# A planned instruction order searched again with other prices, and half of a permuting copy's writes in memory order

## The chip, the cores and the metric

The kernel runs on one core of a Trainium2 chip. The metric is device time in microseconds (us) of one execution. A core has five instruction queues that concern us: PE (TensorE, matmuls), DVE (VectorE), ACT (ScalarE), POOL (GpSimd) and SP (SyncE, which here issues DMAs). Each queue runs in order: an instruction whose inputs are late holds up all that stand behind it on the same engine. Queues wait for one another through semaphores.

## The reference

Attention with random features (Performer), then a Fourier mix and an MLP with a residual. All data is 32-bit float; batch 8, 8 heads, 576 rows, head size 64, 128 features, model width 512, MLP width 2048.

```python
def phi(x):                       # for q and k, scaled by D**-0.25
    h = x @ omega.T - sum(x * x) / 2
    return exp(h - max(h)) / sqrt(m)
kv = phi(k).T @ v                 # per head, over the 576 rows
num, den = phi(q) @ kv, phi(q) @ sum(phi(k))
x = num / (den + 1e-6)            # heads side by side: (8, 576, 512)

u = x + real(fft2(x))             # over rows and columns
un = (u - mean(u)) / sqrt(var(u) + 1e-6)
out = u + relu(un @ w_ch1) @ w_ch2
```

The weights come as 64-bit floats and are narrowed on the chip.

## The kernel before

The program has two parts, and each engine runs all of its first part before its second.

The first part interleaves several streams. Three of them are attention: the 32 pairs of heads are dealt to them in turn (`attn`). One pair takes these steps, and they return in the views below by their lines:

- SP loads K, Q (L375, L378) and V (L383). PE transposes the 9 column blocks of 128 (L511); ACT evicts them from PSUM to SBUF as `kqT`, 512 or 128 columns at a time (L521).
- PE multiplies by the features in quarter tiles (L593). DVE takes the negated maximum of each row (L537), and ACT the exponential with it as a bias, 18 instructions of 128x128 for a pair (L554).
- PE forms `kv` (L627), which DVE or ACT evicts (L641, L643).
- PE transposes the query's features (L511 again) in three groups: one column block, four, and four. ACT evicts each group as `qeT` with a permutation of columns, in two instructions (L528): two of 128x64 and four of 128x256 for a pair.
- PE forms numerator and denominator (L674, L682). DVE takes the reciprocals (L691, L692) and then either DVE multiplies in one instruction (L703) or ACT does it in ten small ones (L699).

Beside attention run: the Fourier mix of a batch as soon as its four pairs are done (folds on DVE and POOL at L730 to L766, PE at L786, L796, L836, L847, ACT at L809 and L880, sums at L897 and L898), the narrowing of 32 weight pieces (L436 or L438, then L441 to L454), the MLP on the first four blocks of 128 rows as filler for PE (L1032, L1055), sums of weight parts (L1125, L1183), and the norms of row blocks (`norm_of`, L962 to L976).

The second part does the rest of the MLP with a product scheme that needs fewer multiplications (PE at L1239 and L1419, sums on DVE, POOL and ACT).

What sets the order is neither the order of the source nor a scheduler's priorities. Every stream is a generator that yields `Step` objects before it records instructions. A `Step` names its engine (or two from which one is chosen) and a planned length in us, the events it needs, and the buffers and PSUM banks it takes and gives back. `Listing.run` keeps a planned clock of each engine and picks, again and again, which stream takes its next step; the instructions are then recorded in that order, and each engine's queue has them so. In the first part the picks are not made greedily: they are written out in the string `PICKS`, one character a step. Its value is split by `divmod(…, 36)`: the remainder is the number of the waiting stream that goes next, and the quotient says whether the step takes the engine that the plan thinks is later, where there are two. The planned lengths still decide which of two engines counts as the earlier and which PSUM bank is free first. In the second part there are no picks, and the step that could begin first by the plan, plus its bias, goes next.

The planned lengths are constants in the source. For the eviction of `qeT` and `kqT` by ACT, for example (`order` is given for `qeT` alone):

```python
cost = 0.05 + 0.107 * (j1 - j0) + (0.06 if order else 0.0)
```

The permuted eviction (`evicted`, L515 to L528) walks the group of four column blocks (`j0` of 1 or 5; h, s, t = 4, 2, 16) with one instruction for each value of s. Its loops are column block, h, t, from the outside to the inside. In SBUF a column block is one float apart, t four floats and h 128; in PSUM t is two floats apart, h 32 and a column block 128.

Of the kernel before, what the change touches and what calls it, by code (L numbers as in the profile page):

```python
# [14 lines left out]
AF = mybir.ActivationFunctionType  # L15
# [20 lines left out]
PE, ACT, DVE, POOL, SP, NONE = "pe", "act", "dve", "pool", "sp", "none"  # L36
# [3 lines left out]
class Clock(NamedTuple):  # L40
# [20 lines left out]


PICKS = (
    "ff40d10e3cdaeebfcdfc3ffcedce8dceajii0ii8b8989i9i827fjejPdgfjhjeejhgidgjiih7cTIhdhOhbfgcbbgggbcggggdh"
    "ciecdhjccikdghddceh9k88lk7hb9aOa8khHM97egcagaba77eiieefileeg8Teffddihhddghhi9cdhicgggccicglgdfcchecf"
    "gcb8ji7hih8hebai89ffgj1GeGf66ggbbegdfefaegffOefcH776dahi6jjjTgfjjKe7jfjj6d6gk6ddkgjmddgiiiijdfbgfhhd"
    "jefjifkkbaOlcjmbkk9hkdj89eofppmhlelmpKLbqdppKn7nlllhfgbgkfijidlkgd9fefijb8dR69j7i7jb8kimkjjnajlhhnjh"
    "cjnjhlkihljgighhU9hhSlmijhjfjmfgaa8obo8nm08kk64ba7nMka8i89k7aegghf6bicheghhfd5gccfhbegh5aibhk3ghfb96"
    "4g79lkfcag7hj87iicmblkfadlgkkdjkgjjjkic7ehi8Jj5cllkfcgmiklihji6hlWbmDVf9cbjjmlfod9eejnjkjmndonimbjnF"
    "q587nSieikih7mfcjhcleekgfTgkPKIddehdcklb4cclajOjajiibab56fc998dffec7e6i8fbidbcagg77fbag7hh54Q78ghffd"  # L70
    "jfghegfk5dlccmSmffdieleieddlNegRejjjghfchJkfhjjebjdbfijjSeeedf6cij5h7bidgcicbdih9fejchefh9bjkeJcccee"
    "di55jiji5kh7jMl86aahhkUhj8bg665ehkkiimnieoQijQhihflgl6j5he6jejj9jcbhjmmVLN89i9k96kkfUagiiibbgieiQhg7"
    "9gfhf6d64bigebahabgd5hPcfdgffddi6cgkfdmfnbm8fgjbdddlflehcgo9elnhk9K4n5ol5oRmm4faoadmU985iimiaLlhGifl"
    "8flimlmkmfjjjplrijjknklkmmhmkilkkk8aagaekljq7!pdiRmimjkihpiqnZnc3jhg6jkefpglhgomdfdondommopk99ihip9p"
    "h4g5kplebombnjbjlbnomkpkgmk6a65jVP4im8ig7lemd87lk7ll5lajkfd3j6llb6ai5mbLONgYoll85fghifmblk6lefk5bklk"
    "g7ekGJhiggmkmnhPhebfnlnflki5bmehjiihdekk900iieedigibcfgca486ed28edaffaee6aeP69g66ffcehOdagabh62b8ah9"
    "a88eOdfadIb9dcbd8affaa63cdNd8dd2d6d7dcafehdaab6aeadd946dee276e8bdcb7d7FF7c9b8MKfgab4f8da766hb9ddMfea"
    "fdb7b8gbadd8acbdd76ed5caac78cd6a5O9ac5f9bGdccggaih8cdeeae4g6g76aaeG7efdfed46277e5abd4a71735P98f5gN6h"
    "E2K9d2biiikahb9jfflac94lll92772343h44hh5JPg8g3ce44ec4dKN558835186M97a9ab48aaba8abc2d837a87J2996b664a"
    "d7bde4EaOgfffg5gHgbQfI98cefggeff7abbK3dea4dbbebac4d42fPb82ee9c7645ad8daaef8f9Nd47hhcbhbh12EHh4Q11ddN"  # L80
    "PfPff0g28G428d34239a99c99ca9099J998aaa5156K98879658bcd9c8Ib85678J7808968006aD50482DIH47753289G86ab6b"
    "49874baa3b33366598063886J69F322022246666664D412332010"
)


# [195 lines left out]
def kernel(  # L281
# [10 lines left out]
    nc = tc.nc  # L292
# [183 lines left out]
    uh = [dram.tile([32, 8, DM], F32, name=f"uh{b}") for b in range(B)]  # L476

    def warm():
        yield Step(PE, 2.5, take=("bank",))
        b, ps = got()  # L480
        for _ in range(6):
            nc.tensor.matmul(ps[:, 0:128], lhsT=ur1[:, 0:128], rhs=ur1[:, 0:128])
        yield Step(NONE, give=(b,))

    def first():

        yield Step(NONE, 3.8)
        yield Step(PE, 0.3, take=("bank",))
        b, omps = got()
        nc.tensor.transpose(omps[:, 0:128], om2d, ident[:])  # L490
        yield Step(DVE, 0.2, makes="om2", give=(b,))
        nc.vector.tensor_scalar(om2[:], omps[:, 0:128], SCALE, None, op0=ALU.mult)
# [20 lines left out]
        return dst  # L513

    def evicted(dst, b, j0, j1, makes, order):  # L515
        cost = 0.05 + 0.107 * (j1 - j0) + (0.06 if order else 0.0)
        yield Step(ACT, cost, 0.02, makes=makes + (j0,), give=(b,), bias=0.08)
        ps = psum_of(b)[:, 0 : 128 * (j1 - j0)].rearrange("q (c p) -> q c p", p=128)
        dst = dst[:, j0:j1, :]
        if order is None:  # L520
            nc.scalar.activation(out=dst, in_=ps, func=AF.Copy)  # L521
            return
        h, s, t = order[j0]
        dst = dst.rearrange("q c p -> q (c p)").rearrange("q (h s t c) -> q s c h t", h=h, s=s, t=t)
        ps = ps.rearrange("q c (h t s) -> q s c h t", h=h, s=s)
        for i in range(s):
            of = ps[:, i, ::-1, :, ::-1] if i and j0 else ps[:, i]
            nc.scalar.activation(out=dst[:, i], in_=of, func=AF.Copy)  # L528

    def softmax(n, ts, num, b, es):  # L530

# [183 lines left out]
    def mix(b):  # L715
# [7 lines left out]
        def folds(n):  # L723
# [11 lines left out]
            for dst, src in ((h[:, 0:NL], h[:, 0:NL]), (h[:, NL : NL + 1], x[:, 4:5])):  # L735
                nc.vector.tensor_tensor(
                    out=dst[:, :, 1 : 2 * QD],
# [7 lines left out]
            for dst, o in ((NC3, ALU.add), (1, ALU.subtract)):  # L745
# [4 lines left out]
                    op=o,  # L750
                )
            step = Step(
                {DVE: 1.02, POOL: 2.5},
                makes=("fold", b, n), give=("half",), port=True, bias=-1.41,
            )
            yield step
# [196 lines left out]
    def norm_of(j, t, i, pool, dst):  # L953
# [4 lines left out]
        st = small.tile([P, 6], F32, name="st", tag="st")  # L958
        mv = small.tile([P, 2], F32, name="mv", tag="mv")
        rstd = small.tile([P, 1], F32, name="rstd", tag="rstd")  # L960
        yield Step(DVE, 1.01, bias=-0.23)
        nc.vector.bn_stats(out=st[:], in_=u[:])  # L962
        nc.vector.bn_aggr(out=mv[:], in_=st[:])
        nc.vector.tensor_scalar(rstd[:], mv[:, 1:2], 1e-6, None, op0=ALU.add)  # L964
        yield Step(POOL, 0.85, port=True, bias=-0.18)
        nc.gpsimd.tensor_tensor(rstd[:], rstd[:], mhalf[:], op=ALU.pow)  # L966
        yield Step(DVE, 0.455, port=True)
        nc.vector.tensor_scalar(u[:], u[:], mv[:, 0:1], rstd[:], op0=ALU.subtract, op1=ALU.mult)
# [588 lines left out]
```

## Time and profile before

The program ran in 1197.02 us, the median of three runs (1194.09 to 1198.68). The profiled execution took 1197.83 us.

| | |
|---|---|
| profiled execution | 1197.83 us |
| its span, first to last instruction of the profile | 1196.0 us |
| PE's first matmul of the second part (L1239) | 438.84 us after the start of the span |
| ACT, permuted copies of 128x256 (L528), x128 | 70.4 us busy, mean 732 ns |
| ACT, permuted copies of 128x64 (L528), x64 | 12.8 us busy, mean 294 ns |
| ACT, exponentials (L554), x576 | 163.9 us busy, mean 449 ns; waited 24.8 us for DVE's maximum (L537) |
| granted TensorE clock | 1.00 throughout |

How to read it. PE's busy time counts modelled ends of pipelined matmuls, so that a busy PE is not yet one at its peak; the weight loads (PEld) beside it show more. Busy time of a group is the union of its instructions, and instructions of one engine overlap at their ends: the mean duration of the 128 long copies times 128 is more than their busy time. What an instruction costs its engine is better read as the time from its start to the next one's start. In timelines a row is a run of equal instructions: start, length of the run, engine, line, operation, tiles, count, and in brackets the idle time before it. "Issue" in the chain of waits is time in which the engine waited for nothing that the profile shows.

### The profile page before, as it was taken

How to read it: one execution, taken by the hardware profiler on the slowest of the kernel's cores; microseconds unless marked ns; L12 is line 12 of the kernel's file. 1: busy time of each engine (PE TensorE's matmuls, PEld its weight loads, DVE VectorE, ACT ScalarE, POOL GpSimd, SP SyncE). 2: the span in 40 equal slices, each digit the busy share in tenths (PEclk: the TensorE clock that was granted, in tenths of full speed). 3: DMA queues.
4: the chain of work that ended last, by engine and by line, in shares of the span. 5: the costliest groups of instructions: out<-in, count | busy, mean ns of one | idle time of the engine just before them, and what ended most of it. 6: DMA issues, size and time to landing. Idle time of an engine off the chain costs nothing.

```text
span 1196.0 us, 31842 instructions
## 1 busy us (share of the span) xinstructions
PE 1169.7 (98%) x12765; PEld 1044.3 (87%) x12765; DVE 710.7 (59%) x1508; ACT 486.0 (41%) x1562; POOL 418.3 (35%) x484
## 2 busy tenths in 40 slices
PE   8989999999999999999999999999999999999998
PEld 6778788778868768998998998999899899899898
DVE  5889899796557562672572473374275176267245
ACT  7989899877755112222222222222222222222211
POOL 2444554363453205304314323322421431430421
PEclk9999999999999999999999999999999999999999
DMA  8745856467564342682483384295096086177255
GB/s 257 211 140 179 243 165 187 127 195 223 143 208 147 107 131 93 199 261 79 154 288 97 109 295 135 63 299 177 13 305 198 32 268 200 63 228 248 62 158 196
DMA packets 144708, 205.71 MB, mean 172 GB/s; under 512 B 49072, under 2 KB 58544, under 8 KB 144560
## 3 DMA queue, kind: packets, MB, share of 16 engines
q1 hardware_dynamic: 144064, 203.41, 53.9%
q8 instruction: 101, 1.65, 0.6%
q14 instruction: 47, 0.39, 0.1%
q10 hardware_dynamic: 496, 0.26, 0.1%
HBM read 171.90 MB, written 35.91 MB: 174 GB/s over the span
## 4 chain that ended last, share of the span: by engine, by line
PE 85%; ACT 9%; DVE 3%; issue 1%; DMA 1%; SPq 1%; POOL 0%; DVEq 0%; ACTq 0%; POOLq 0%
PE banks L1239 32%; PE banks L1419 29%; ACT e L554 5%; PE banks L1032 4%; PE banks L1055 4%; PE banks L511 3%; PE banks L593 3%; ACT qeT L528 2%; PE banks L674 2%; PE banks L627 1%; PE banks L972 1%; PE banks L786 1%; PE banks L836 1%; ACT kqT L521 1%; PE banks L796 1%
## 5 line engine op out<-in xcount | busy, mean ns | idle before, releaser
L1225 DVE CUSTOM_DVE_ANT_0 hid<-banks,s 128x256 f32<-128x256 f32 x192 | 79.7, 423 | 255.3 <-PE banks L1239 250.5
L1419 PE MATMUL banks<-wl,sums 128*128 128x128 f32 x1792 | 217.3, 275 | 0.0
L1419 PEld LDWEIGHTS banks<-wl,sums 128*128 128x128 f32 x1792 | 208.8, 192 | 0.4
L1253 ACT ACTIVATE s<-banks 128x256 f32<-128x256 f32 x192 | 73.8, 384 | 262.9 <-PE banks L1239 262.9
L554 ACT ACTIVATE e<-banks,nmx 128x128 f32<-128x128 f32 x576 | 163.9, 449 | 25.0 <-DVE nmx L537 24.8
L1239 PE MATMUL banks<-unT,w 128*128 128x256 f32 x704 | 167.5, 379 | 0.0
L1239 PEld LDWEIGHTS banks<-unT,w 128*128 128x128 f32 x704 | 132.7, 190 | 17.9 <-issue 0.5
L1394 ACT ACTIVATE s<-banks 128x128 f32<-128x128 f32 x168 | 46.6, 278 | 242.3 <-PE banks L1419 195.7
L1239 PE MATMUL banks<-tt,w1s 128*128 128x256 f32 x512 | 126.2, 379 | 0.0
L1306 POOL TENSOR_TENSOR hs<-hid 128x256 f32<-128x256 f32 x64 | 46.5, 727 | 208.8 <-DVE hid L1225 178.8
L1239 PEld LDWEIGHTS banks<-tt,w1s 128*128 128x128 f32 x512 | 97.3, 190 | 13.2
L537 DVE TENSOR_REDUCE nmx<-banks 128x8 f32<-128x1024 f32 (+1 forms) x96 | 89.8, 952 | 27.7 <-PE banks L593 26.2
L1399 DVE TENSOR_TENSOR part<-banks,s 128x128 f32<-128x128 f32 x168 | 48.8, 291 | 88.6 <-PE banks L1419 88.0
L1419 PE MATMUL banks<-wl,hid 128*128 128x128 f32 x768 | 97.6, 275 | 0.0
L1419 PEld LDWEIGHTS banks<-wl,hid 128*128 128x128 f32 x768 | 93.5, 192 | 1.2
L1306 POOL TENSOR_TENSOR hs<-hid,hs 128x256 f32<-128x256 f32 x64 | 46.6, 729 | 119.9 <-issue 94.9
L593 PE MATMUL banks<-om,kqT 64*64 64x128 f32 x2304 | 81.3, 275 | 6.1 <-ACT qeT L528 2.3
L528 ACT ACTIVATE qeT<-banks 128x256 f32<-128x256 f32 (+1 forms) x192 | 81.1, 586 | 9.2 <-PE banks L511 8.7
L1239 PE MATMUL banks<-unT,w1s 128*128 128x256 f32 x320 | 80.7, 379 | 0.0
L593 PEld LDWEIGHTS banks<-om,kqT 64*64 64x64 f32 x2304 | 64.3, 133 | 18.1 <-issue 6.7
L966 POOL TENSOR_TENSOR rstd<-rstd,mhalf 128x1 f32<-128x1 f32 x36 | 24.5, 680 | 147.4 <-DVE rstd L964 146.4
L1419 PE MATMUL banks<-wl,hs 128*128 128x128 f32 x576 | 74.9, 275 | 0.4 <-DVE part L1399 0.4
(128 smaller groups left out, 1978.3 us busy)
## 6 DMA issues: line engine op xcount, KB each, us to landing
wl<-w2l SPq DMA_DIRECT2D x392, 256.0 KB, 3.7
raw<-in_moe_w_ch_dram SPq DMA_DIRECT2D x32, 512.0 KB, 5.6
vd<-in_v_dram SPq DMA_DIRECT2D x32, 288.0 KB, 4.6
kq<-in_k_dram SPq DMA_DIRECT2D x32, 288.0 KB, 4.3
kq<-in_q_dram SPq DMA_DIRECT2D x32, 288.0 KB, 4.8
u<-us SPq DMA_DIRECT2D x36, 256.0 KB, 4.0
ur<-us SPq DMA_DIRECT2D x36, 256.0 KB, 3.8
out_dram<-ur SPq DMA_DIRECT2D x34, 256.0 KB, 2.5
```

What stands on the lines that cost most here:

```text
L528: nc.scalar.activation(out=dst[:, i], in_=of, func=AF.Copy)
L537: nc.vector.tensor_reduce(nmx[:, :, 0:num], pps[:, :, 0 : MF * num].rearrange("p b (c m) -> p b c m", m=MF), axis=AX.X, op=ALU.max, negate ...
L554: nc.scalar.activation(out=e[:, c + (i if num == 1 else 0), :], in_=pps[:, i, MF * c : MF * c + MF], func=AF.Exp, bias=nmx[:, i, c : c + 1],)
L593: nc.tensor.matmul(pps[cols, c, MF * m : MF * m + MF], lhsT=kqT[rows, j, cols], rhs=om2[rows, :],)
L1032: nc.tensor.matmul(hp[:, 0:TP], lhsT=w1[:, dc, 128 * fc : 128 * fc + 128], rhs=unTs[key][:, dc, :], start=(dc == 0), stop=(dc == NDC - 1),)
L1055: nc.tensor.matmul(yp[:, 0:DM], lhsT=hs[fc][:, 128 * i : 128 * i + 128], rhs=w2[:, fc, :], start=(fc == 0), stop=(fc == NFC - 1),)
L1225: nc.vector._custom_dve(TENSOR_ADD_SAT, out=o, in0=ps, in1=sb, s0=FMAX, s1=0.0)
L1239: nc.tensor.matmul(ps[:, 0:HT], lhsT=left(dc), rhs=right(dc), start=start and dc == 0, stop=(dc == D2 - 1), skip_group_check=True,)
L1253: nc.scalar.activation(out=s[:], in_=ps[:, 0:HT], func=AF.Copy)
L1306: nc.gpsimd.tensor_tensor(out=o, in0=l, in1=r, op=op)
L1399: nc.vector.tensor_tensor(out=part[:, t, 128 * m : 128 * m + 128], in0=ps[:, 0:128], in1=saved[with_][:], op=ALU.add,)
L1419: nc.tensor.matmul(ps[:, 0:128], lhsT=left[:, f], rhs=wls[j, i, n][:, f], start=start and f == 0, stop=(f == 3), skip_group_check=True,)
```

## The change

Four things are edited. The string `PICKS` is another one (1853 characters before and after; nearly every row of it differs). Planned lengths of several steps are others: the warm-up, the first step, the permuted eviction, the last step of a fold, and two steps of the norm. In the permuted eviction, the group that begins at column block 1 walks its loops in the order h, t, column block instead of column block, h, t, so that its writes go through SBUF in the order of memory; the group that begins at 5 and the single block keep the old loop order. What is computed stays the same.

```diff
 PICKS = (
-    "ff40d10e3cdaeebfcdfc3ffcedce8dceajii0ii8b8989i9i827fjejPdgfjhjeejhgidgjiih7cTIhdhOhbfgcbbgggbcggggdh"
...
+    "ff40d00d3cacfgdbgce3gbbcecccegc8cbabfhg0iiii8ef9a89h827edhOiicfhedidjhggciee7ebhJhceadafaedafffbbffb"
...
 )
@@ def warm():
-        yield Step(PE, 2.5, take=("bank",))
+        yield Step(PE, 1.37, take=("bank",))
@@ def first():
-        yield Step(NONE, 3.8)
+        yield Step(NONE, 2.65)
@@ def evicted(dst, b, j0, j1, makes, order):
-        cost = 0.05 + 0.107 * (j1 - j0) + (0.06 if order else 0.0)
+        cost = 0.01 + 0.222 * (j1 - j0) if order else 0.05 + 0.107 * (j1 - j0)
...
         for i in range(s):
-            of = ps[:, i, ::-1, :, ::-1] if i and j0 else ps[:, i]
-            nc.scalar.activation(out=dst[:, i], in_=of, func=AF.Copy)
+            of, to = ps[:, i, ::-1, :, ::-1] if i and j0 else ps[:, i], dst[:, i]
+            if j0 == 1:
+                of, to = (a.rearrange("q c h t -> q h t c") for a in (of, to))
+            nc.scalar.activation(out=to, in_=of, func=AF.Copy)
@@ def mix(b): folds(n), the last step
-                {DVE: 1.02, POOL: 2.5},
+                {DVE: 1.2, POOL: 2.2},
@@ def norm_of(j, t, i, pool, dst):
-        yield Step(DVE, 1.01, bias=-0.23)
+        yield Step(DVE, 1.12, bias=-0.23)
...
-        yield Step(POOL, 0.85, port=True, bias=-0.18)
+        yield Step(POOL, 1.05, port=True, bias=-0.18)
```

The step's number of instructions is the same in all of these; only the eviction's access patterns are others. Which engine takes a step with two engines follows from the picks: in the new program ACT has 80 of the small multiplications at L699 for 40 before, DVE 24 of those at L703 for 28, ACT 16 of the weight steps at L438 for 19 and POOL 16 at L436 for 13. Two more lines of source put each line number behind L526 up by two in the new program.

## The prediction

> **What bounds the kernel now.** I read the page's busy shares first, then the busy time by stage, then the chain of waits, then the timeline of ACT and PE. The program has two parts: attention, mixing and the first four row blocks of the MLP (until PE's first L1239), then the rest of the MLP. The page and the timeline of PE:
>
> ```profile
> span 1196.0 us, 31842 instructions
> PE 1169.7 (98%) x12765; PEld 1044.3 (87%) x12765; DVE 710.7 (59%) x1508; ACT 486.0 (41%) x1562; POOL 418.3 (35%) x484
> ...
> 425.10 13.90 PE L1055 MATMUL banks<-w,ht 128*128 128x512 f32 x32
> 438.84 1.03 PE L1239 MATMUL banks<-unT,w 128*128 128x256 f32 x4
> ```
>
> The second part starts at 438.84 and takes 1196.0 - 438.84 = 757.2 us. By stage (columns: stretch, its length, then busy us and instructions of PE, PEld, DVE, ACT, POOL; granted clock, DMA share, GB/s):
>
> ```profile
> 0.00:40.00 40.00, 33.84 (x797) 27.94 (x801) 24.19 (x41) 31.97 (x104) 14.09 (x19) 1.00 0.84 248
> 40.00:69.00 29.00, 26.65 (x559) 21.50 (x551) 26.65 (x50) 28.21 (x101) 10.00 (x8) 1.00 0.52 144
> 69.00:120.00 51.00, 46.92 (x1104) 40.62 (x1102) 43.59 (x110) 43.07 (x141) 26.40 (x29) 1.00 0.63 187
> 120.00:160.00 40.00, 37.88 (x876) 33.08 (x875) 33.74 (x65) 34.96 (x119) 21.75 (x17) 1.00 0.68 211
> 160.00:200.00 40.00, 38.93 (x820) 33.85 (x821) 37.58 (x88) 36.89 (x128) 17.02 (x15) 1.00 0.61 176
> 200.00:257.00 57.00, 53.50 (x1036) 42.65 (x1037) 47.90 (x107) 46.41 (x150) 23.09 (x24) 1.00 0.57 171
> ...
> 390.00:439.00 49.00, 49.00 (x281) 33.66 (x278) 25.65 (x72) 7.26 (x22) 7.80 (x12) 1.00 0.29 85
> ...
> 700.00:800.00 100.00, 99.96 (x685) 93.82 (x684) 52.22 (x112) 22.41 (x67) 30.55 (x40) 1.00 0.55 178
> ```
>
> The second part is PE's alone: weight loads fill 93.8 of 100 us and PE is idle for 0.04. Until 257 us three engines are loaded together: ACT 221.5 of 257 us (86%; 97% from 40 to 69), DVE 213.7 (83%), PE idle 19.3 by the sum of its column. From 257 to 439 PE is idle only 2.1 us more. So what can be won lies in the first 257 us, in waits of PE on ACT, DVE and loads. The chain of waits in the stretch up to 260 us says whose:
>
> ```profile
> by line: ACT e L554 18.4%; ACT qeT L528 9.5%; PE banks L511 8.9%; PE banks L593 8.9%; PE banks L674 6.9%; issue 4.5%; PE banks L1032 4.2%; ACT kqT L521 3.8%; PE banks L627 3.7%; PE banks L1055 3.5%; DMA kq<-in_q_dram 3.1%; DMA raw<-in_moe_w
> ```
>
> ACT is the engine that sets the pace most often there. The timeline of ACT gives what a copy really holds the engine for (start to next start; the durations overlap):
>
> ```profile
> 66.97 0.30 ACT L521 ACTIVATE kqT<-banks 128x128 f32<-128x128 f32 x1
> 67.13 2.10 ACT L528 ACTIVATE qeT<-banks 128x256 f32<-128x256 f32 x4
> 68.95 1.16 ACT L554 ACTIVATE e<-banks,nmx 128x128 f32<-128x128 f32 x4
> ...
> 99.23 0.35 ACT L528 ACTIVATE qeT<-banks 128x64 f32<-128x64 f32 x2
> 99.44 2.21 ACT L554 ACTIVATE e<-banks,nmx 128x128 f32<-128x128 f32 x8
> ...
> 109.75 0.60 ACT L976 ACTIVATE unT<-banks 128x512 f32<-128x512 f32 x1
> 110.25 3.08 ACT L528 ACTIVATE qeT<-banks 128x256 f32<-128x256 f32 x6
> ```
>
> A plain copy of 128 columns takes 0.16, of 512 columns 0.50, so one of 256 lies at 0.16 + (0.50 - 0.16)/3 = 0.27. The permuted ones of 256 take 1.82/4 = 0.455 each, the permuted ones of 64 columns 0.21/2 = 0.105, which is on the plain line. So a pair of long permuted copies holds ACT 0.91 us, where the plan of before prices it at 0.05 + 0.107 x 4 + 0.06 = 0.54: 64 such pairs, 24 us of ACT that the plan did not know of.
>
> **What the Trainium skill says.** "Advanced Engine Details and Errata", Memory Cachelines: SBUF has 16-byte lines, a run of accesses needs two hits on a line to go at full speed, and a new line at each access is penalised; PSUM's lines have 8 bytes. Before, the long copies write every fourth float, a new SBUF line at each element; the excess of 0.455 - 0.27 = 0.185 us over 256 elements fits it. The short copies (h, s, t = 2, 2, 32, one column block) read every second float, a new PSUM line each time, and are not slow: for ACT the trace shows no price on the PSUM side. "Perfetto Trace Analysis", Identifying Dependency Chains: an instruction that waits for several engines may get semaphore instructions put before it. The trace has these, at 17 ns each for ACT where nothing is late.
>
> **The change part by part.**
>
> The copy's loop order (j0 == 1: two of the four long copies of each of 32 pairs, 64 copies). Writes become runs of 64 floats, four to a line; reads step by 512 bytes, a new PSUM line each, as before. If the write side is the cause, a copy falls from 0.455 to 0.27: 64 x 0.185 = 11.8 us of ACT work less. Bounds: nothing (the cause is the read side) to all of it; below nothing if the long read step costs, which no row shows. How much reaches the end: L528 stands on the chain with 6.7% of the 420 us that I asked for, 28.1 us, of its 81.1 us busy (page's group), a share of 0.35. 11.8 x 0.35 = 4.1 us. What is late next there is DVE's L537, which ACT already waited 24.8 us for, so not more. Taken: -4; ends 0 and -9.
>
> The new order of the first part. The two built programs have the same 6745 matmuls; the MLP filler (L1032, L1055) and the mixing stand at the same places among the pairs: pair 24's last product has 217 us of PE work ahead of it in both (217.0 and 217.5, by 0.109 per transpose, 0.23 per four of L593 and so on). Switches between groups of different tile shape rise from 227 to 235, at about 0.1 us (a step from L511 to L593 is 0.20 where one within L511 is 0.11): +0.8. Work ahead of the evictions of pair 20, by the same spacings: ACT 181.2 before, 179.9 after by order alone, 172.9 with the faster copies; DVE 197.3 and 196.2 by summed durations. Over the whole part ACT gets four more of L699's groups of ten (4 x 10 x 0.2 = +8.0) and three fewer of L438 (-1.7), DVE four fewer of L703 (-3.3), POOL three more of L436 (+4.7). All four of the added L699 groups stand behind pair 22, where PE has filler and the slack is ACT's: cost nothing; without that cover up to 8.0 x 0.35 = 2.8. POOL is busy under half of the time: its share is hidden. The first loads: K goes ahead of V on SP's queue, so it is issued 0.76 us earlier (0.72 for 1.48), but Q stays third and the first L593 stands behind Q's transposes: 0. The tables (eight DMAs) now go in front of the third V and later weight pieces on SP; PE's uses of both are far away: 0. Waits on PE in this part fall from 704 to 674: 30 x 17 ns, 0.5 at most.
>
> What is left of the order is how well each queue's head is ready when its turn comes. Removable is PE's idle time of 19.3 us before 257 us less about 6 that precede the first data: 13 us. A plan that prices ACT at 0.90 for a pair where 0.91 is measured should place PE's steps behind ready evictions more often; I take a third, -4. Ends: -10, and +5 if the new queues block one another where the old ones did not.
>
> The other prices (fold, bn_stats, the power, warm) put no instruction in or out. They shift the second part's order, which has no picks: 14 additions of L1459 go from DVE (0.69) to POOL (1.27), +17.8 us on an engine at 30%; nothing of PE's waits on them soon. The last 263 matmuls stand alike. PE's 752.7 us of issue stay: 0, ends -0.5 and +1.5. Its inputs are early: the last L1100 ends at 427.4, 11 us ahead of its use.
>
> Sum: -4 - 4 = -8, so a profiled execution of 1197.83 - 8 = 1189.8 (span 1188, second part from 430.8). The median of the runs is 0.8 below the profiled one: 1189.0.
>
> **The rivals.**
>
> (a) The order pays more: most of the 13 us of idle goes and the copies pay 6: -15, 1182. For it: ACT stood at 97% from 40 to 69 us and the missing price was 24 us. Against: DVE at 83% takes over.
>
> (b) The freed ACT time is hidden: PE's order and DVE's L537 set the pace, and local waits only move. -1, 1196. For it: DVE's work ahead of pair 20 changes by only 1.1 us, PE's not at all. Against: the chain has ACT on it for a third of that stage.
>
> (c) Slower: the strided PSUM read of the reordered copies is slow. At 0.70 us a copy ACT gets (0.70 - 0.455) x 64 = 15.7 us, of which at least half reaches the end since ACT then stands near 92% before 257 us: +8, while the order, planned for 0.90 a pair, gains nothing as its 1.40 breaks it: 1205. It decides from 0.64 a copy, at which the loss reaches 6. For it: the skill names short PSUM lines. Against: the 64-column copies.
>
> (d) The change doesn't do what it says: the copies are unchanged at 0.455 and only the order counts: -3, 1194.
>
> **How the numbers follow.** Within 0.5% means 1191.0 to 1203.0, about what a measurement of this kernel can tell from no change. My forecast (-8, own range 1184 to 1193) 0.46; (a), 1177 to 1184, 0.20; (b) 0.15; (c) 0.09; (d) 0.10. Faster: three quarters of the forecast, all of (a), a tenth of (b) and (d): 0.345 + 0.20 + 0.025 = 0.57. Slower: most of (c) and a little of an order that blocks: 0.10. Same: 0.33. The range from 1179 to 1198 leaves out (c) and the far end of (a).
>
> **What would show it.** PE's first L1239 near 431 and the same 757 us behind it; the 128x256 copies in two kinds, a pair at 0.91 and one near 0.55; ACT's share before 257 us a few points lower, and L528 lower on the chain. Wrong: the reordered copies at 0.45 or more; a second part that grows by over 1.5 us; ACT's waits on L537 growing by as much as the copies give.

## The result and the profile after

The changed kernel runs in 1191.32 us, the median of seven runs (1189.02 to 1192.05), against 1197.02 (1194.09 to 1199.95) before: a ratio of 0.995 with a 95% interval of 0.9932 to 0.9967. It is a little faster, by 5.7 us: the interval stays below one and the two ranges don't meet. The profiled execution took 1192.05 us, 5.8 less than the one of before. The page's head, and from the timeline of PE the start of the second part (L1241 is the L1239 of before):

```profile
span 1190.2 us, 31894 instructions
PE 1166.4 (98%) x12765; PEld 1043.5 (88%) x12765; DVE 689.0 (58%) x1482; ACT 484.1 (41%) x1602; POOL 457.2 (38%) x506
...
428.42 1.03 PE L1241 MATMUL banks<-unT,w 128*128 128x256 f32 x4
```

The first part ends at 428.42 for 438.84: 10.4 us won. The second part takes 1190.2 - 428.42 = 761.8 us for 757.2: 4.6 lost. So the small net gain is the difference of two larger effects. Busy time by stage (same columns as before: stretch, length, busy us and instructions of PE, PEld, DVE, ACT, POOL, granted clock, DMA share, GB/s):

```profile
0.00:40.00 40.00, 32.84 (x741) 27.53 (x741) 24.57 (x41) 29.96 (x101) 12.12 (x18) 0.96 0.83 243
40.00:69.00 29.00, 27.09 (x606) 21.86 (x598) 26.50 (x52) 27.21 (x102) 11.22 (x8) 1.00 0.54 151
69.00:120.00 51.00, 48.03 (x1113) 41.20 (x1111) 44.51 (x107) 41.63 (x143) 29.06 (x31) 1.00 0.65 187
120.00:160.00 40.00, 37.49 (x883) 32.65 (x882) 33.23 (x62) 35.59 (x122) 22.62 (x20) 1.00 0.68 210
160.00:200.00 40.00, 39.93 (x836) 35.26 (x836) 38.75 (x92) 35.87 (x132) 18.59 (x16) 1.00 0.64 191
200.00:257.00 57.00, 57.00 (x1117) 45.37 (x1116) 51.38 (x115) 48.70 (x168) 28.18 (x27) 1.00 0.59 176
...
700.00:800.00 100.00, 98.96 (x674) 92.63 (x673) 48.62 (x103) 23.94 (x69) 35.06 (x43) 1.00 0.54 173
```

From 160 to 257 us PE is idle for 0.07 us (before for 1.1 in the first 40 of these and 3.5 in the other 57). In the first 40 us it is idle longer than before (32.84 busy for 33.84), it has issued 741 matmuls for 797, and the clock shows 0.96. From 700 to 800, in the second part, PE is idle for 1.0 us where it was idle for 0.04. The whole first part in one row each, before and then after:

```profile
0.00:438.84 438.84, 417.46 (x7726) 341.13 (x7726) 328.76 (x706) 315.84 (x1055) 179.57 (x175) 1.00 0.58 176
```
```profile
0.00:428.42 428.42, 413.00 (x7725) 339.39 (x7726) 318.72 (x694) 311.69 (x1095) 190.93 (x183) 1.00 0.60 180
```

PE's idle time falls from 438.84 - 417.46 = 21.4 to 15.4, by 6.0 us. The other 4.5 us come out of its busy time, with the same matmuls (7726 and 7725 records). So busy time is not a fixed amount of work, and the idle column alone understates what can be won. Short waits inside runs of instructions, which don't show as idle, are the likely reason; no run here shows it.

The long permuted copies (two groups of 64, the first 64 in memory order), and the chain of waits up to 260 us:

```profile
L530 ACT ACTIVATE qeT<-banks 128x256 f32<-128x256 f32 x128 | 59.0, 599 | 2.8 <-PE banks L511 2.5
```
```profile
by line: PE banks L595 11.6%; ACT e L556 11.5%; PE banks L511 9.8%; PE banks L629 5.9%; PE banks L676 5.5%; DMA kq<-in_q_dram 5.4%; DMA raw<-in_moe_w_ch_dram 4.1%; DVE nmx L539 3.9%; issue 3.6%; PE banks L1057 3.4%; PE banks L1034 3.3%; PE 
```

Their busy time fell from 70.4 to 59.0 us, and qeT, the second on the chain of before with 9.5%, is no longer among its first eleven. PE's own lines lead it, and the load of a weight piece (raw) has gone up from 3.1% or less to 4.1%.

From start to next start (medians where ACT goes on at once), a copy in memory order holds ACT for 0.265 to 0.285 us. The old ones hold it, in before, for 0.426 (the first copy of a group) and 0.479 (the second, which reads in reversed order). The prediction's estimate of a plain copy of 256 columns was 0.27.

### The profile page after: what moved, and what is told of

Same layout as the page of the kernel before. It is cut to its first block, busy times and chain, and to the rows that moved or that the text cites. A ratio compares the mean times of both kernels' runs of the same rounds, so it can differ in the third digit from the quotient of the medians.

```text
span 1190.2 us, 31894 instructions
## 1 busy us (share of the span) xinstructions
PE 1166.4 (98%) x12765; PEld 1043.5 (88%) x12765; DVE 689.0 (58%) x1482; ACT 484.1 (41%) x1602; POOL 457.2 (38%) x506
## 4 chain that ended last, share of the span: by engine, by line
PE 87%; ACT 4%; DVE 4%; DMA 2%; issue 1%; SPq 1%; POOL 0%; DVEq 0%; ACTq 0%; POOLq 0%
PE banks L1241 33%; PE banks L1421 29%; PE banks L1034 5%; PE banks L1057 4%; PE banks L595 4%; PE banks L511 4%; ACT e L556 3%; PE banks L629 2%; PE banks L676 2%; PE banks L838 1%; PE banks L788 1%; DMA kq<-in_q_dram 1%; PE banks L974 1%; DVE nmx L539 1%; DMA raw<-in_moe_w_ch_dram 1%
## 5 line engine op out<-in xcount | busy, mean ns | idle before, releaser
L556 ACT ACTIVATE e<-banks,nmx 128x128 f32<-128x128 f32 x576 | 165.1, 447 | 17.8 <-DVE nmx L539 17.2
L1241 PE MATMUL banks<-unT,w 128*128 128x256 f32 x704 | 168.6, 379 | 0.0
L1241 PEld LDWEIGHTS banks<-unT,w 128*128 128x128 f32 x704 | 132.2, 190 | 17.5 <-issue 0.5
L1241 PE MATMUL banks<-tt,w1s 128*128 128x256 f32 x512 | 125.0, 379 | 0.0
L1241 PEld LDWEIGHTS banks<-tt,w1s 128*128 128x128 f32 x512 | 97.2, 190 | 13.3
L539 DVE TENSOR_REDUCE nmx<-banks 128x8 f32<-128x1024 f32 (+1 forms) x96 | 89.3, 951 | 24.8 <-PE banks L595 22.3
L1241 PE MATMUL banks<-unT,w1s 128*128 128x256 f32 x320 | 79.5, 379 | 0.0
L968 POOL TENSOR_TENSOR rstd<-rstd,mhalf 128x1 f32<-128x1 f32 x36 | 29.9, 832 | 128.7 <-DVE rstd L966 128.7
L595 PEld LDWEIGHTS banks<-om,kqT 64*64 64x64 f32 x2304 | 63.3, 133 | 15.2 <-issue 4.6
L530 ACT ACTIVATE qeT<-banks 128x256 f32<-128x256 f32 (+1 forms) x192 | 69.3, 504 | 7.2 <-PE banks L511 6.9
```

Source lines behind the costliest of these rows:

```text
L530: nc.scalar.activation(out=to, in_=of, func=AF.Copy)
L539: nc.vector.tensor_reduce(nmx[:, :, 0:num], pps[:, :, 0 : MF * num].rearrange("p b (c m) -> p b c m", m=MF), axis=AX.X, op=ALU.max, negate ...
L556: nc.scalar.activation(out=e[:, c + (i if num == 1 else 0), :], in_=pps[:, i, MF * c : MF * c + MF], func=AF.Exp, bias=nmx[:, i, c : c + 1],)
L595: nc.tensor.matmul(pps[cols, c, MF * m : MF * m + MF], lhsT=kqT[rows, j, cols], rhs=om2[rows, :],)
L1241: nc.tensor.matmul(ps[:, 0:HT], lhsT=left(dc), rhs=right(dc), start=start and dc == 0, stop=(dc == D2 - 1), skip_group_check=True,)
```

## The experiments

The theory at the outset: copies and order both shorten the first part and pay in part for the same waits, and the 4.6 us of the second part come from the norm's prices, which reorder it. The rivals: the copies carry the whole gain of the first part, or the order does; the second part is longer by the state in which the first one leaves it.

All runs are compared with the kernel before on the same chip (its medians there: 1195.8 to 1196.8; small differences between runs of two chips are therefore taken from the distances to before). "First part" is the start of PE's first L1239 or L1241 in the profiled execution; the second part is the rest of the span.

| run | median us (range) | ratio to before (95%) | first part | second part |
|---|---|---|---|---|
| e1_strided | 1192.29 (1191.39–1193.31) | 0.9959 (0.9941–0.9976) | 429.22 | 761.8 |
| e2_mem_old_order | 1188.72 (1187.15–1190.88) | 0.9933 (0.9917–0.9950) | 431.87 | 757.1 |
| e3_norm_old | 1186.44 (1186.00–1187.61) | 0.9917 (0.9902–0.9933) | 428.61 | 757.1 |
| e5_all_mem_norm_old | 1185.81 (1185.20–1186.96) | 0.9912 (0.9895–0.9928) | 426.21 | 757.1 |
| e6_norm_new | 1202.28 (1199.97–1203.51) | 1.0046 (1.0031–1.0062) | 437.86 | 761.9 |
| e7_middle_loop | 1196.73 (one run) | – | 437.70 | 757.2 |
| e8_all_mem_old_order | 1186.10 (1184.76–1187.50) | 0.9911 (0.9896–0.9926) | 427.72 | 757.1 |
| e10_act_moved | 1202.39 (1201.15–1205.48) | 1.0048 (1.0030–1.0066) | 443.50 | 757.4 |
| e11_act_undone | 1192.52 (1190.29–1194.73) | 0.9960 (0.9945–0.9974) | 428.68 | 762.0 |
| e12_tables_later | 1183.89 (1183.14–1184.73) | 0.9901 (0.9886–0.9916) | 424.23 | 757.2 |
| e13_tables_later_all_mem | 1184.37 (1182.08–1185.54) | 0.9899 (0.9884–0.9914) | 424.30 | 757.1 |
| e14_adds_dve | 1185.67 (1185.37–1186.38) | 0.9909 (0.9885–0.9934) | 425.80 | 757.7 |

How far a first part of one profiled execution can be trusted: kernels with the first part of before give 438.84, 437.86 (e6) and 437.70 (e7); their mean, 438.1, is used below. The slow copies of e7 count among them since they are the ones of before in time. Kernels with the first part of after give 428.42, 428.61 (e3) and 425.80 (e14), a spread of 2.8 us. A difference of this size between two first parts proves nothing; there the medians decide, and they too have some noise: e6, whose first part is that of before, comes out about 1 us longer by them than its second part explains. The second part repeats within 0.3 us.

### Which of the two parts wins the first 10 us

The new order with the old loop order of all copies:

```diff
-            if j0 == 1:
+            if False:
                 of, to = (a.rearrange("q c h t -> q h t c") for a in (of, to))
```

> The new order with the old loop order in all copies. Theory A (the order and the copies each give part): the first part, 428.4 us in the changed kernel, grows by 64 x 0.15 us of ACT times the share 0.35 of it on the chain, about 3 to 4 us, to 432; the second part stays at 761.8; total 1195. Theory B (the copies carry nearly all of the 10.4 us): first part 437 to 439, total 1201. Theory C (the order carries it all, ACT's freed time is hidden): first part 428 to 429, total 1191.

And the old order with the new loop order of the same 64 copies:

```diff
-            of = ps[:, i, ::-1, :, ::-1] if i and j0 else ps[:, i]
-            nc.scalar.activation(out=dst[:, i], in_=of, func=AF.Copy)
+            of, to = ps[:, i, ::-1, :, ::-1] if i and j0 else ps[:, i], dst[:, i]
+            if j0 == 1:
+                of, to = (a.rearrange("q c h t -> q h t c") for a in (of, to))
+            nc.scalar.activation(out=to, in_=of, func=AF.Copy)
```

> The kernel before, with only the 64 copies' loop order changed. Theory A: first part from 438.8 to about 435, second part unchanged at 757.2, total 1193. Theory B: first part near 430, total 1188. Theory C: first part 438 to 439, total 1197. In every case the 64 copies should hold ACT about 0.30 us each where they held it 0.455.

Measured: the copies alone end the first part at 431.87, 6.3 us earlier than 438.1; the order alone at 429.22, 8.9 earlier; both together at 428.42, 9.7 earlier. The two gains don't add (15.2 against 9.7). On the new order the copies give 0.8 us (1.6 by the medians), less than the spread, and the times of after and e1 overlap. None of the three theories holds for both orders: e1 comes nearest to C, and e2 lies between A and B. The groups of the copies in e1 and e2 (busy us, mean ns of one, then the idle time before them):

```profile
L530 ACT ACTIVATE qeT<-banks 128x256 f32<-128x256 f32 x128 | 73.2, 748 | 3.0 <-PE banks L511 2.6
```
```profile
L530 ACT ACTIVATE qeT<-banks 128x256 f32<-128x256 f32 x128 | 56.0, 577 | 5.7 <-PE banks L511 5.1
```

The copies did in e1 and e2 what they do in before and after: ACT is relieved of 14.2 us by the one edit on the new order (73.2 to 59.0) and of 14.4 on the old (70.4 to 56.0). It is the use of the freed time that differs. The chain of waits in e1, from 160 to 215 us, says why:

```profile
by line: PE banks L511 23.0%; PE banks L595 19.5%; PE banks L676 11.9%; PE banks L629 10.3%; PE banks L1034 9.2%; PE banks L838 8.6%; PE banks L788 6.3%; PE banks L798 5.4%; PE banks L849 4.1%; PE banks L684 2.5%
```

Every line there is PE's, even with the slow copies: the new order already places them behind work of PE. In before, the same view from 160 to 220 us begins with the copy:

```profile
by line: ACT qeT L528 14.2%; PE banks L674 10.6%; PE banks L593 10.4%; PE banks L511 9.2%; PE banks L1032 8.4%; ACT e L554 6.2%; PE banks L627 5.8%; issue 5.6%; PE banks L836 4.0%; PE banks L786 3.6%; PE banks L796 3.3%; ACT kqT L521 2.7%; 
```

The times at which a pair's last product (of L674 and L682, counted in the trace) starts tell where each gain comes up:

| pair | before | after | e1 (order alone) | e2 (copies alone) |
|---|---|---|---|---|
| 4 | 50.8 | 52.3 | 54.3 | 51.8 |
| 8 | 84.0 | 84.0 | 86.2 | 83.4 |
| 12 | 136.3 | 136.7 | 137.0 | 134.3 |
| 16 | 176.5 | 175.3 | 175.6 | 173.5 |
| 20 | 219.7 | 214.5 | 214.7 | 214.1 |
| 24 | 281.9 | 274.9 | 275.2 | 276.0 |
| 28 | 326.5 | 319.6 | 320.4 | 319.6 |
| 32 | 389.9 | 379.7 | 380.5 | 382.9 |

Until pair 12 the new order wins nothing, in e1 it is behind. It wins from pair 12 to 24 and again behind pair 28. The copies alone win from pair 8 on, first by little.

### Where the 4.6 us of the second part come from

The new kernel with the norm's two prices of before in the second part only:

```diff
-        yield Step(DVE, 1.12, bias=-0.23)
+        yield Step(DVE, 1.12 if listing.clock is FIRST else 1.01, bias=-0.23)
...
-        yield Step(POOL, 1.05, port=True, bias=-0.18)
+        yield Step(POOL, 1.05 if listing.clock is FIRST else 0.85, port=True, bias=-0.18)
```

> The changed kernel with the old planned lengths of the norm's two steps (1.01 and 0.85) in the second part alone; its second part's matmul order is then that of the kernel before. Theory D (the longer second part comes from the norm's prices): second part 757 us, first part as in the changed kernel at 428.4, total 4.5 us less than the changed kernel, 1186.5. Rival E (it comes from starting the second part earlier, with its inputs or memory traffic less ready): second part stays near 761.5, total 1191.

And the reverse, before with the new prices in the second part only:

```diff
-        yield Step(DVE, 1.01, bias=-0.23)
+        yield Step(DVE, 1.01 if listing.clock is FIRST else 1.12, bias=-0.23)
...
-        yield Step(POOL, 0.85, port=True, bias=-0.18)
+        yield Step(POOL, 0.85 if listing.clock is FIRST else 1.05, port=True, bias=-0.18)
```

> The kernel before with the new planned lengths of the norm's two steps in the second part alone; its second part's matmul order is then that of the changed kernel. Theory D: first part as before at 438.8, second part 761.5 to 762, with a wait of PE of about 0.5 us for DVE's normalised rows in each of seven blocks; total 1201.5. Rival E: second part 757, total 1197.

Measured: e3 takes 757.1 us for the second part and 1186.44 in all, 4.9 less than after (4.3 by the distances to before); e6 takes 761.9 and 1202.28, slower than before, with the whole interval above one. Theory D holds in both runs. The start of the second part differs by 9 us between the two and plays no part: it is the two prices, in both directions. PE's waits in the second part, of after and then of e3 (engine, line, what it waited for: us in all, times, longest):

```profile
PE banks L974 <- DVE u L970: 3.5, 7, 0.5
...
PEld banks L974 <- DVE u L970: 4.8, 7, 0.7
```
```profile
PEld banks L974 <- DVE u L970: 1.6, 7, 0.2
```

One of the seven places, in the timeline of DVE and PE in after (start, length, engine, line, operation, tiles, count, and in brackets the idle time ahead):

```profile
510.37 1.27 DVE L1388 TENSOR_TENSOR sums<-hid,sums 128x512 f32<-128x512 f32 x1 [0.44 <-PE banks L1421]
511.57 0.54 DVE L970 TENSOR_SCALAR u<-u,mv,rstd 128x512 f32<-128x512 f32 x1
...
510.17 0.60 PE L974 MATMUL banks<-ident,u 128*128 128x128 f32 x4
510.60 1.06 PE L1421 MATMUL banks<-wl,sums 128*128 128x128 f32 x8
512.16 0.65 PE L974 MATMUL banks<-ident,u 128*128 128x128 f32 x4 [0.50 <-DVE u L970]
```

The same two row blocks in before:

```profile
520.78 0.99 DVE L968 TENSOR_SCALAR u<-u,mv,rstd 128x512 f32<-128x512 f32 x2
...
521.37 1.11 PE L972 MATMUL banks<-ident,u 128*128 128x128 f32 x8
```

Before, DVE scales two row blocks one behind the other and PE transposes both together. After, the plan counts the norm's steps as longer and puts an addition (L1388) between the two; PE's second four transposes stand in its queue ahead of the next MLP products and wait 0.50 us, seven times. PE is idle 761 - 752.78 = 8.2 us of the second part (windows from 429 to 1190) for 757 - 752.11 = 4.9 before; these 3.3 us are about the 3.5 of the waits, and the rest of the 4.6 lies inside busy time.

Two readings were left: the split of the transposes is to blame, or the addition between, which takes 1.27 us where the same addition takes 0.68 elsewhere. At that moment POOL runs one of the additions that went over to it (L1461):

```profile
509.83 1.27 POOL L1461 TENSOR_TENSOR ur<-ur,part 128x512 f32<-128x512 f32 x1 [2.45 <-ACT part L1454]
```

It ends at 511.10, and DVE's ends at 511.64, 0.54 later: as if DVE's had stood still until POOL was through. All seven places look so. Before has such blocked additions at seven places too (1.00 us each), but no wait of PE's matmuls behind them. "SBUF — State Buffer", two separate sides, in the Trainium skill, says that DVE's instructions with two SBUF inputs share a pair of ports with GpSimd (POOL here), that the one that starts first holds it for its whole instruction, and that the other blocks. Where DVE comes first the trace has it the other way round, DVE at its 0.68 and POOL at 1.66 for 1.27:

```profile
497.34 0.68 DVE L1388 TENSOR_TENSOR sums<-hs 128x512 f32<-128x512 f32 x1
497.49 1.66 POOL L1461 TENSOR_TENSOR ur<-ur,part 128x512 f32<-128x512 f32 x1 [1.68 <-ACT part L1454]
```

The test is after with these additions kept on DVE (POOL then has 23 of them, for 39 in after and 25 in before). PE's order stays that of after, four transposes and four, with the addition of L1388 between the two scalings:

```diff
-            step = Step({POOL: 1.35, DVE: 0.7}, port=True, **kw, bias=0.06)
+            step = Step({DVE: 0.7} if i in (5, 6) else {POOL: 1.35, DVE: 0.7}, port=True, **kw, bias=0.06)
```

> The changed kernel with the additions of L1461 for the products 5 and 6 kept on DVE in every block, as in the kernel before; PE's order stays that of the changed kernel, with the transposes of L974 split four and four. Reading A: DVE's addition at L1388 ahead of the second L970 takes 1.27 us for 0.68 because an addition of L1461 runs on POOL at the same time; with none there it falls to 0.68, L970 comes about 0.6 earlier, the seven waits of 0.50 go, and the second part takes 757 to 758.5 us, about 1187.5 in all. Reading B: the split of the transposes with the addition between is enough; L1388 stays at 1.27 or the wait stays, and the second part takes 761 to 762 us, about 1191 in all.

The same place in e14:

```profile
507.55 0.60 PE L974 MATMUL banks<-ident,u 128*128 128x128 f32 x4
507.75 0.69 DVE L1388 TENSOR_TENSOR sums<-hid,sums 128x512 f32<-128x512 f32 x1 [0.43 <-PE banks L1421]
508.36 0.54 DVE L970 TENSOR_SCALAR u<-u,mv,rstd 128x512 f32<-128x512 f32 x1
508.95 0.66 PE L974 MATMUL banks<-ident,u 128*128 128x128 f32 x4
```

Reading A: the addition takes 0.69, no wait of L974 is left, the second part takes 757.7 us, and the whole 1185.67 for 1191.32. The split itself costs at most 0.6 us (757.7 against 757.1). So the way from the price to the loss is: longer norm steps in the plan, another place for the additions, 14 of them on POOL, seven of these beside an addition of DVE that they block, DVE's next step late by 0.6 us, PE late by 0.5. Which of the two prices sets this off is not shown: the runs change both together.

### Where a long copy loses its time, and how many copies matter

Before, with the loops of the 64 copies as h, column block, t: the writes keep their step of 16 bytes from element to element, the other loops change places.

```diff
+                of, to = (a.rearrange("q c h t -> q h c t") for a in (of, to))
```

> The kernel before with the 64 copies in the loop order h, column block, t: other outer loops, but the innermost loop still writes every fourth float. Theory I (a new SBUF line at each written element is what costs): the copies stay at 0.455 us each, total 1197. Rival J (the outer loops or the read order are what costs): the copies fall toward 0.30, total near 1190.

Before, with all 128 long copies in memory order (`if j0:` in place of `if j0 == 1:`):

```diff
+            if j0:
+                of, to = (a.rearrange("q c h t -> q h t c") for a in (of, to))
```

> The kernel before with all 128 long copies in memory order, order and planned lengths untouched. Theory F: the first 64 copies gave 6.5 us; the other 64 give less, since the end of the first part closes up to the 428 us where PE paces: first part 428 to 430, total 1185.5 to 1188. Rival G (the gain goes with ACT's time): another 6.5 us, first part near 425, total 1182. Rival H (the order, not PE's own work, keeps it up): no further gain, first part 431 to 432, total 1188.7.

The groups of e7 and e8:

```profile
L530 ACT ACTIVATE qeT<-banks 128x256 f32<-128x256 f32 x128 | 70.2, 729 | 4.7 <-PE banks L511 4.3
```
```profile
L530 ACT ACTIVATE qeT<-banks 128x256 f32<-128x256 f32 x128 | 41.8, 427 | 6.1 <-PE banks L511 5.3
```

e7's copies are as slow as those of before (70.4 busy there; e7's spacing is 0.42 and 0.48): the outer loops don't matter, so theory I holds. That it is the innermost step of the write and not that of the read, which is 8 bytes in all slow copies, rests on the short copies of 64 columns: they read at that same step, write without gaps, and aren't slow (0.105 us in the prediction). "Advanced Engine Details and Errata", Memory Cachelines, in the Trainium skill, says that SBUF's lines have 16 bytes and that a different line at each access is penalised, without a size; here it is 0.15 to 0.2 us for 256 elements. Its warning that reads of PSUM with gaps are slow is worded for matmuls; ACT reads at steps of 512 bytes with no loss in e8 (0.264 us).

e8 ends the first part at 427.72: the second 64 copies give another 4.2 us on the old order (2.7 by the medians), about as theory F had it. So the edit of the copies alone, on the old order (1186.10), gives the first part as much as the search and half of the copies (428.42), and it leaves the second part alone.

The same with the new order and the second part's old prices:

```diff
-            if j0 == 1:
+            if j0:
```

> The new order, all 128 long copies in memory order, and the norm's old planned lengths in the second part. Theory F (in the new order PE itself paces the first part, so that ACT's time is covered): another 10 us less of ACT moves the first part's end by less than 1 us from 428.6; second part 757; total 1185.5 to 1187. Rival G (ACT still paces, and the small effect of the first 64 copies on the new order was an accident of their places): first part near 425, total 1182 to 1183.

The first part ends at 426.21 for e3's 428.61: more than theory F's 1 us, but within the spread. The total, 1185.81 for e3's 1186.44, lies in theory F's range and not in rival G's, and the ranges of e5 and e3 overlap. Again the copies count for less on the new order.

### The multiplications that moved to ACT

On the old order, L699 given to ACT for the same eight pairs as in after (six pairs move to ACT and two back to DVE, four more in all):

```diff
-        step = Step({DVE: 0.74, ACT: 1.97}, give=(ndb,), makes=("x", b, pr), bias=-0.07)
+        step = Step({ACT: 1.97} if n in (4, 15, 21, 22, 24, 27, 30, 31) else {DVE: 0.74}, give=(ndb,), makes=("x", b, pr), bias=-0.07)
```

> The kernel before, with the multiplication by the reciprocal done by ACT for the pairs for which the changed kernel has it on ACT (4, 15, 21, 22, 24, 27, 30, 31 instead of 4, 15, 20, 28); PE's order is untouched. Theory K (these moves are what the new order gains behind pair 20): pair 32's last product 3 to 5 us earlier than 389, total 1192 to 1193. Rival L (the gain comes from the order of the queues, the moves are covered or even cost ACT time): pair 32 at 389 or later, total 1196 to 1199.

On the new order, four of the eight groups given back to DVE:

```diff
+        step = Step({ACT: 1.97} if n in (4, 15, 21, 27) else {DVE: 0.74}, give=(ndb,), makes=("x", b, pr), bias=-0.07)
```

> The changed kernel with four of its eight such multiplications (pairs 22, 24, 30, 31) back on DVE; PE's order is untouched. Theory K: the first part's end goes from 428.4 back to 431.5 or more, total 1194 to 1196. Rival L: it stays at 428 to 429, total 1191.

e11 is as after (428.68 and 1192.52): rival L holds there, and the move costs nothing. e10 ends its first part at 443.50, 5.4 later than 438.1 and worse than both theories had it. PE's group of L593 in e10, and two windows that meet at 258.92 us:

```profile
L593 PE MATMUL banks<-om,kqT 64*64 64x128 f32 x2304 | 81.6, 278 | 5.2 <-ACT qeT L528 2.3 <-ACT kqT L521 1.5 <-ACT x L699 1.4
```
```profile
255.51:258.92 3.41, 1.75 (x42) 1.27 (x42) 1.94 (x5) 3.41 (x14) 3.12 (x4) 1.00 0.68 211
258.92:262.33 3.41, 3.40 (x32) 2.41 (x33) 1.30 (x2) 1.03 (x5) 3.13 (x3) 0.50 0.61 154
```

There the moved work holds up PE: two waits for L699, of 0.75 and 0.60 us, stand at 257 to 259 us, and TensorE's clock is at one half behind them. This explains a part only. PE's idle time in the whole first part is 21.5 us for 21.4 in before, so most of the loss lies inside its busy time; the half clock can be 1.7 us of it, and the rest was not located. Still, "covered" is a property of the order: the same 8 us of ACT are free in one and cost 5.4 in the other.

### What the new order loses in its first 40 us

The pair times show the new order behind by 1.5 to 3.5 us at pair 4 in after and e1. The longest waits of PE in the first part of after:

```profile
PE banks L676 <- DVE kv L643: 3.0, 1, 3.0
PE banks L511 <- DMA kq<-in_q_dram: 2.0, 4, 0.9
```

The first is one wait, a fifth of all idle time that is left. What made DVE late, from the timeline of DVE and then of PE:

```profile
26.79 0.43 DVE L441 TENSOR_SCALAR sign<-raw 128x512 uint32<-128x512 uint32 x1 [1.96 <-DMA raw<-in_moe_w_ch_dram]
28.66 0.69 DVE L443 SCALAR_TENSOR_TENSOR w<-w,sign 128x512 uint32<-128x512 uint32 x1 [1.44 <-POOL w L436]
...
32.59 0.28 DVE L643 COPY kv<-banks 128x130 f32<-128x130 f32 x1
...
32.93 2.00 PE L676 MATMUL banks<-kv,qeT 128*64 128x65 f32 x32 [3.03 <-DVE kv L643]
```

A weight piece comes late; DVE waits for it, then for POOL's step on it; the copy of kv, which has nothing to do with the weights, stands behind both in DVE's queue, and PE waits for the copy. The piece is late since the new order has put eight table loads ahead of it on SP's queue. Then the clock: two windows of after, and two of e1.

```profile
29.14:32.55 3.41, 0.76 (x36) 0.51 (x27) 3.38 (x5) 1.40 (x5) 1.51 (x1) 1.00 0.67 251
32.55:35.97 3.42, 3.04 (x43) 2.93 (x44) 2.81 (x9) 2.86 (x12) 1.97 (x1) 0.50 0.36 100
```
```profile
31.21:34.62 3.41, 1.83 (x86) 1.41 (x80) 3.23 (x5) 2.70 (x9) 1.64 (x2) 1.00 0.99 352
34.62:38.04 3.42, 2.05 (x45) 1.79 (x46) 3.35 (x9) 2.83 (x13) 1.75 (x1) 1.00 0.29 78
```

With the idle 3.03 us (from 29.90 to 32.93) TensorE's clock falls to one half until about 36. A fall does not need so long a wait: it came in e14 behind one of 1.95 us and in e10 behind several of at most 0.75. In e1 the same wait is 2.17 us, cut in two by the windows above, and no fall followed. (The clock column also shows 1.00 where the profile has no record of the clock, as at the very start: in e12 L515's transposes stand 213 ns or more apart until about 8 us and 109 from 10 us on. So "1.00 throughout" in the table of before is not shown for its first 4.7 us.) The test: e3 with the eight table loads issued behind the fifth weight piece.

```diff
+    late_tabs = []
...
-                nc.sync.dma_start(tab_sb[n][p0:p1], src[p0:p1])
+                late_tabs.append((tab_sb[n][p0:p1], src[p0:p1]))
...
                 nc.sync.dma_start(raw[:].rearrange("p n two -> p (n two)"), src.bitcast(U32))
+                while i == 4 and late_tabs:
+                    nc.sync.dma_start(*late_tabs.pop(0))
```

> The changed kernel with the norm's old planned lengths in the second part, and with the eight table loads issued behind the fifth weight piece instead of behind the second; nothing else is moved. Theory M (the new order puts 0.9 MB of tables ahead of the weight pieces; the third piece then comes late, DVE waits for it with the copy of kv behind it, PE is idle for 3 us near 30 us, and its clock is halved for 3.4 us after that): PE's idle time there goes, no half clock between 30 and 40 us, first part from 428.6 to 424 to 426, total 1182 to 1184. Rival N (the late piece is only one of several that are late at once, or the early lead is lost again in later waits): first part 427 to 429, total 1185 to 1187.

The run takes 1183.89 us for e3's 1186.44. It is 11.9 us below before on its chip, where e3 is 10.0 below and e14, with the same first part as e3, 10.4. So the gain is 1.5 to 2.0 us, and the intervals of the three ratios overlap: by the medians alone it is not clear of noise. The first part of the profiled execution ends at 424.23, 4.4 us before e3's, of which up to 2.8 can be the spread. The profiles speak for it early on: the third weight piece lands at 22.2 us for 26.8 in after, and pair 8's last product starts at 82.1 in e12 and 83.2 in e13, where the six profiles with the tables in their old place (after, e1, e3, e5, e11, e14) have 84.0 to 86.2. The window from 30 to 40 us, of after and then of e12, and e12's copy of kv:

```profile
30.00:40.00 10.00, 7.07 (x162) 6.45 (x162) 9.09 (x16) 7.96 (x29) 5.13 (x4) 0.83 0.61 191
```
```profile
30.00:40.00 10.00, 9.13 (x294) 7.99 (x286) 7.73 (x15) 10.00 (x37) 1.60 (x2) 1.00 0.94 258
```
```profile
31.03 0.29 DVE L647 COPY kv<-banks 128x130 f32<-128x130 f32 x1
```

The half clock and the 3 us of idle time are gone, and PE issues 294 matmuls for 162, as theory M had it. With all long copies in memory order on top (`if j0:`):

> The same with all 128 long copies in memory order. Theory M: first part from 426.2 to 422 to 424, total 1180 to 1182. Rival N: first part 425 to 427, total 1184 to 1186.

1184.37 us, first part 424.30: nothing more to be had from the copies. The total is rival N's and not theory M's. e12 and e13 are the fastest of all, about 1.0% below before (0.9901, interval 0.9886 to 0.9916, for e12), and beat both kernels.

## Why the prediction was right, and where not

The forecast was 1189.0 with a sum of -8 that lay all in the first part; measured are 1191.32 and, in the profiled execution, -10.4 in the first part and +4.6 in the second. The size of the whole came out near by luck, since two steps missed in opposite directions. Of its three outcomes the prediction thought "faster", below 1191.0, the likeliest (0.57); 1191.32 lies 0.3 us on the other side of that line, in what it called the same (0.33).

- *The copies fall from 0.455 to 0.27, 11.8 us of ACT.* Right: 0.265 to 0.285 for 0.426 and 0.479, by spacing (0.4525 - 0.275) x 64 = 11.4 us. That the write side is the cause and the strided read costs nothing was right too (e7, e8 and the short copies); rival (c) and rival (d) fall.
- *A share of 0.35 reaches the end: -4.* Wrong as a constant: 6.3 of 11.4 on the old order (0.55), 0.8 of 11.4 on the new one (0.07, with a spread as large as the effect). The share was read from the chain of before and then used on an order in which the copies aren't on the chain. The wait that was to be the next limit, ACT's for DVE's L537, did not grow: 24.8 us before, 23.0 in e2, 17.2 after.
- *The new order takes a third of 13 us of idle: -4.* Mis-sized: alone it gives 8.9. The bound of 13 us was too low as well, since 4.5 us of the 10.4 came from PE's busy time, and e12's profiled first part is 438.84 - 424.23 = 14.6 shorter than before's. With both edits the sum of -8 was 2.4 short, which the overlap of the two made small.
- *Gains placed before 257 us.* Partly: pair 24's last product starts 7.0 us earlier at 275, but another 3.3 us come behind pair 28, at over 320 us, where I had seen only 2.1 us of idle from 257 on.
- *The extra groups of L699 cost nothing, else 2.8.* Right in the new order (e11), and the price without cover was 5.4, not 2.8 (e10), of which the mechanism is only in part located.
- *The tables go ahead of weight pieces: 0, as PE's uses of both are far away.* Wrong. PE's use is far, DVE's is not: an unrelated eviction stood behind it in DVE's queue. Worth some 1.5 to 2.0 us (e12 against e14 and e3, each by its distance to before; the intervals overlap). The prediction followed the moved transfers to their last user and not to the next instruction in line behind each user.
- *The norm's prices: 0, ends -0.5 and +1.5.* The step that failed: +4.6. I had the cause in hand, the 14 additions that go from DVE (0.69) to POOL (1.27), and wrote that nothing of PE's waits on them soon. That is true of their results. But seven of them hold DVE up while they run (0.68 becomes 1.27), and DVE's next step is awaited by PE's transposes. PE was idle for 0.04 in 100 us, so each such wait is lost in full. e14 puts the additions back and gets 4.1 of the 4.6 us back. A second part that grows by over 1.5 us was what the text said would show it wrong.

Rival (b), that freed ACT time is hidden anyway, describes well what the copies do in the new order, but not in the old. The kernel reaches a time near rival (a)'s 1182 only with the second part and the tables put right (e12, 1183.89). Nothing of the slower rival (c) came about; what did slow the kernel was the part priced at nothing.

Open: which of the two norm prices sets off the second part's order, and why first parts of the same program differ by up to 2.8 us from one execution to the next. The half clock of the first 40 us does not tell them apart: e14 has two stretches of it (6.8 us) where after and e3 have one (3.4), and yet e14 ends first. It gets its lead between pairs 8 and 20 (84.3 and 211.9 us, where after has 84.0 and 214.5, e3 85.4 and 214.3).

## What to carry to other kernels

A share of the chain that you read before an edit holds for the order that it was read in; if order and durations change together, test each alone, for they may pay for the same idle time. A plan's price is an edit of the schedule, and an instruction that it moves to another engine is not priced by who waits for its result alone: look at what the old engine runs beside it, since the two may block each other. And where a transfer is moved, follow it to everything that stands behind its reader in that engine's queue, not only to the use of its data.

## What the runs showed of the hardware

- In memory order an ACT copy of 256 fp32 values out of PSUM holds ACT 0.265 to 0.285 us even though it reads at steps of 512 bytes; with writes at steps of 16 bytes 0.42 to 0.48, whatever the outer loops (e7).
- A DVE addition of 128x512 (L1388) that starts while POOL runs an addition ends 0.54 to 0.55 us behind POOL's: it takes 1.27 us for 0.68 where POOL started 0.54 before it (after), 1.00 where POOL started 0.82 before it (before). Where DVE was first, POOL takes 1.66 to 1.73 for 1.27.
- TensorE's clock fell to one half for 3.41 us ten times in these profiles, their last us apart. In the 3.41 us ahead of a fall PE was idle for 1.66 to 2.66 us in sum: 2.66 in after, 1.95 in e14, 1.66 in e10, where no wait was longer than 0.75. The clock's changes in one execution lie whole multiples of 3.41 us apart, and of the other windows on that grid none passed 1.58 us but one in e3: it had 1.78 and no fall, and the next, with 1.71, was followed by one. e1's wait of 2.17 lay across two windows (1.58 and 1.36 idle). "TensorE: Matmul & The Clock Gate", What's actually happening, in the Trainium skill, puts the fall after one idle window or more of about 3.4 us, free-running: the length and the free-running grid agree, but here a window that was idle for about half of its length was enough. e12 has no such window from 10 to 40 us and keeps a clock of 1.00 there. What share of e12's gain is the clock's and what the wait's was not told apart.
